# A set-attention and feed-forward kernel: the chunk products of the first attention half made eight visits later, its exponential two visits later, and a chooser that links the parts of a late chain and scores its last visit

## The chip, the cores and the metric

The kernel runs on one core of a Trainium2 chip. The metric is the device time of one execution in microseconds, the median over runs. A core has five engines with an instruction stream each: TensorE (PE, matrix products, with its weight loads as PEld), VectorE (DVE), ScalarE (ACT), GpSimd (POOL) and SyncE (SP), which issues most of the DMA transfers here. Each stream runs in the order in which it was written, and the streams meet through semaphores.

## The reference

An array x of 4 batches x 12,480 tokens x 128 channels goes through an induced set attention, and the result, 49,920 tokens, through a feed-forward layer:

```python
def mab(q, kv):
    s = scale * (q @ kv.transpose(0, 2, 1))
    s = s - s.max(-1, keepdims=True)
    a = np.exp(s)
    a /= a.sum(-1, keepdims=True) + 1e-09
    return a @ kv
h = mab(I, x)            # 32 inducing points attend to all tokens of a batch
y = mab(x, h)            # each token attends to the 32 rows of h
hid = y @ w_in           # 128 -> 2048
g = np.maximum(hid, 0.0) + alpha * np.minimum(hid, 0.0)
out = g @ w_out          # 2048 -> 128
```

The first `mab` needs a maximum and a sum over a whole batch before anything of the second can start. The second and the feed-forward layer work token by token.

## The kernel before

**Visits.** The heavy part is the feed-forward layer. A block is 4 tiles of 128 tokens (512 tokens), and the 2048 hidden channels are done in 4 visits of 512 channels, so a block takes 4 visits. There are 390 visits, numbered 0 to 389: 96 for each batch, and 6 for the tokens left over. In a visit (`visit`, L834 and after) PE makes four products `hh` of 128 channels x 512 tokens (L848; the 32 rows of h are folded into the weights as `HW`, so that four products of 32 rows run side by side). Each `hh` fills one of PSUM's eight banks. ACT (L861) or DVE (L863) applies the ReLU and writes it as `gt` in bf16, r = 0 to 3. After the next visit's four `hh`, PE multiplies the four `gt` of the visit before with W1 into a sum `bp` (`second`, L874, sixteen products). The linear part of the PReLU is added for two blocks at once (L901, every eighth visit). When a block's sum is complete, ACT (L927) or DVE (L929) copies it to `ob`, and SP sends it out (L934).

**Side work.** While the visits of batch b run, two other things are made between them. One is the second attention's weights for the next 2048 tokens of the same batch: scores (L684), their copy (L742, L744), maximum (L761), exponential on ACT (L728), sum, reciprocal, product and a DMA transpose `a<-rep` (L806). The other is the first attention of batch b+1, in seven pieces p = 0 to 6 (piece 1 is the short one of 192 tokens). For each piece: a load `xs`, a cast on POOL, a DMA transpose `xT` (L355), four score products (L378, `a_scores`), their scaled minimum on DVE (L417, L427), an exponential on ACT (L443, `e1T`), a factor for the running minimum (`fac`, L461), a DMA transpose of the exponentials (`e<-e1T`, L474), sixteen products with the tokens (L498, `a_h`) and their addition to the running sum `hs` on DVE (L512, L523). At the end of the seven pieces a chain closes the batch: `mg` (L542), `rb` (L551), `m` and `mf` (L558 to L564), `ex` on ACT (L577), `dx` and `den` on DVE (L587, L590), a product with `den` (L607), `rec`, a product with `hs` (L622), `hT` and the folded weights `HW` (L638, L645).

**Tables and the chooser.** The table near the end of the kernel names the visit after which each of these steps is written: `score`, `look` (the exponential; the transpose one visit and the factor two visits after), `join` (the products `a_h` and the addition). The class `Plan` then walks once over all visits before anything is written. For each visit it knows the side work's engine steps as a chain of (engine, ns) pairs, and it chooses with a beam of 64 states: which engine does which of the four ReLUs, which engine copies a finished block, whether a chain's ACT and DVE part is written at once or *late* (in the next visit, between its second and third ReLU), and which PSUM bank each product takes. `step` adds up a model of the engines' times with fixed prices (`RELU`, `COPY`, `FREE`, `SEM`), and `choose` keeps the states with the smallest estimated end of PE. The order of every engine is what these choices give. The lists `late` and `waits` carry the late parts from one visit to the next.

Of the kernel before, what the change touches and what calls it, by code (L numbers as in the profile page):

```python
# [30 lines left out]
def kernel(  # L31
# [55 lines left out]
    whole_pieces = pieces_of([(0, 0, ST), short, *((s, 0, ST) for s in range(1, NS - 1))])  # L87
# [26 lines left out]
    class Plan:  # L114
# [41 lines left out]
        def step(self, state, n, relus, ways):  # L156


            pe, a, v, e1, free, held, late = state
            cols, linear, accs, last, chains = self.visits[n]  # L160
            busy = {"a": a, "v": v}
            free, held, used = list(free), dict(held), []

            def take(pe):
                k = min(range(BANKS), key=lambda k: max(free[k] + self.SEM, pe))
                used.append(k)
                pe = max(pe, free[k] + self.SEM)
                free[k] = self.NEVER
                return pe, k

            hh, mine = [], []
            for r in range(R):
                k = min(range(BANKS), key=lambda k: free[k])
                used.append(k)
                mine.append(k)
                pe = max(pe, free[k] + self.SEM) + 4
                free[k] = self.NEVER
                hh.append(pe + cols * 0.417 + self.ARRIVE)
            out = []
            for r in range(R):  # L180
                if r == 2:
                    for k, ns, ready, bank in late:
                        busy[k] = max(busy[k], ready) + ns
                        if bank is not None:
                            free[bank] = busy[k] + 100
                lat, per, over = self.RELU[relus[r]]
                out.append(max(busy[relus[r]], hh[r]) + lat + per * cols)
                free[mine[r]] = out[r]
                busy[relus[r]] = out[r] - over
            pe += cols * 0.417  # L190
            for k in accs[0]:
                if k not in held:
                    pe, held[k] = take(pe)
            pe += linear + self.MODE
            for k in accs[1]:
                if k not in held:
                    pe, held[k] = take(pe)
            for r in range(R):
                pe = max(pe, e1[r] + self.SEM) + last * self.FREE
            waits = []  # L200
            for chain, way in zip(chains, ways):
                ready, bank = 0, None
                for kind, ns in chain:
                    if kind == "!":
                        continue
                    if kind == "free":
                        free[ns] = ready + 100
                        continue
                    if kind == "acc":
                        ready, bank = pe + self.ARRIVE, held.pop(ns)  # L210
                        continue
                    if kind in "ps":
                        if kind == "s":
                            pe, bank = take(pe)
                        pe += ns
                        ready = pe + self.ARRIVE
                        continue
                    k = way[0] if kind == "f" else kind
                    ns = self.COPY[k] if kind == "f" else ns
                    if way[-1:] == "l":  # L220
                        waits.append((k, ns, ready, bank))
                    else:
                        busy[k] = ready = max(busy[k], ready) + ns
                        if bank is not None:
                            free[bank] = ready + 100
                    bank = None
                if bank is not None:
                    free[bank] = ready + 600
            new = pe + self.MODE, busy["a"], busy["v"], tuple(out), tuple(free)
            return (*new, tuple(held.items()), tuple(waits)), used  # L230

        def choose(self):
# [3 lines left out]
            for n, (*_, chains) in enumerate(self.visits):  # L236
                ways = []
                for chain in chains:
                    kinds = [k for k, _ in chain]
                    if "f" in kinds:  # L240
                        ways.append([e + w for e in "av" for w in "nl"])
                    elif "!" in kinds or not {"a", "v"} & set(kinds):
                        ways.append([""])
                    else:
                        ways.append(["n", "l"])
                found = {}
                for state, path in beam:
                    for way in product(*ways):
                        for relu in relus:
                            new, used = self.step(state, n, relu, way)  # L250
                            at = new[0] + 390
                            over = max(new[1] - at, 0) + max(new[2] - at, 0)
                            over += sum(w[1] for w in new[6]) * 0.3
                            score = new[0] + 0.3 * over
                            ends = sorted(max(x - new[0], -200) for x in new[4])
                            key = (
                                *(int(x - new[0]) // 16 for x in new[1:3] + new[3]),
                                *(int(x) // 16 for x in ends if x < self.NEVER / 2),
                                new[6],
                            )  # L260
                            if key not in found or score < found[key][0]:
                                found[key] = (score, new, (path, relu + "".join(way), used))
                best = sorted(found.values(), key=lambda f: f[0])[: self.WIDTH]
                beam = [(new, path) for _, new, path in best]
# [8 lines left out]
    plan = Plan()  # L273
# [959 lines left out]
    end = State()  # L1233
# [27 lines left out]

    for b, s, nt in groups[1:]:
        n = first[b, s]
        when = [n - 23, n - 19, n - 16, n - 14, n - 13, n - 11, n - 9, n - 6]
        if (b, s) == (0, 1):
            when = [0, 2, 3, 6, 7, 9, 9, 9]
        if (b, s) == (0, 2):
# [32 lines left out]
    for b in range(B - 1):  # L1300
# [3 lines left out]
        for p, pc in enumerate(whole_pieces):  # L1304
            m = n + (8 * (p - 1 + (not b and p > 2)) if p > 1 else p)
            load, cast, turn = m - 3, m + 6, m + 8
            score = m + 15 if p > 1 else n + 16
            look = score + 1 + (p == 1)
            join = m + (24 if p == whole_pieces[-1].k else 23) if p > 1 else n + (31 if p else 23)
            if not b:  # L1310
                load, cast, turn = {
# [1 line left out]
                }.get(p, (load, cast, turn))  # L1313
                score, look = (score, look) if p > 1 else (score + 4, look + 4)
                join = n + 31 if p < 2 else n + 39 if p < 3 else join
            f = pc.full
            if load >= 0:
                at(load, on, b + 1, a_load, pc)
# [32 lines left out]
    for n, (blk, i) in enumerate(visits):  # L1351
# [3 lines left out]
        if i == 0 and n > NV:  # L1355
# [6 lines left out]
        plan.visits.append(  # L1362
            (blk.nt * blk.per * P, cost, (both, [before.k] if n else []), nt, chains)
        )
    plan.choose()

    prev = None
# [49 lines left out]
```

## Time and profile before

| | |
|---|---|
| median of 3 runs | 591.42 us (591.18 to 591.59) |
| the profiled execution | 593.02 us, of which the span of instructions 591.1 us |
| PE busy | 580.7 us, 98% of the span |
| PEld busy | 436.2 us, 74% |
| DVE busy | 534.4 us, 90% |
| ACT busy | 536.8 us, 91% |
| POOL busy | 217.2 us, 37% |
| granted TensorE clock | full speed in all slices |

How to read it: the busy share of PE counts each product until its modelled end, so small waits between products hide in it. They show better in the starts of the `hh` products of successive visits. The last group of sixteen L874 products of a visit starts about a third of a microsecond after its `hh`, and the next `hh` follow about a microsecond later. A visit that carries side work on PE is longer by that work.

### The profile page before, as it was taken

What the parts mean: (1) busy time and instruction counts of PE and PEld (TensorE: products, weight loads), DVE (VectorE), ACT (ScalarE), POOL (GpSimd) and SP (SyncE); (2) the same over time, 40 slices, a digit from 0 to 9 for tenths busy, and PEclk for the clock granted to TensorE, in tenths of its full rate; (3) what the DMA queues carried; (4) which work ended last, traced back from release to release, by engine and by line L of the source; (5) the groups of instructions that cost most, each with busy time, mean ns of one, the idle gap of its engine ahead of it and who ended that gap; (6) DMA issues with size and microseconds to landing.
All of it is one profiled execution on the core that took longest, in us unless ns stands there. A gap on an engine that the chain in (4) does not pass through costs nothing.

```text
span 591.1 us, 23015 instructions
## 1 busy us (share of the span) xinstructions
PE 580.7 (98%) x9443; PEld 436.2 (74%) x9443; DVE 534.4 (90%) x974; ACT 536.8 (91%) x1085; POOL 217.2 (37%) x259
## 2 busy tenths in 40 slices
PE   7899999999999999999999999999999999999997
PEld 3577777777777777777777777777777777777776
DVE  5799999988998998999999899999999999999996
ACT  5699999999999999999998999999999998999986
POOL 3575552523325426313226256124034134144110
PEclk9999999999999999999999999999999999999999
DMA  8786799734188899432256999741331331441321
GB/s 334 252 213 169 153 256 217 116 91 74 38 240 185 184 205 222 103 82 70 77 151 176 216 216 221 143 99 38 92 75 54 91 81 48 118 85 58 91 69 48
DMA packets 121964, 80.56 MB, mean 136 GB/s; under 512 B 103761, under 2 KB 105729, under 8 KB 118785
## 3 DMA queue, kind: packets, MB, share of 16 engines
q1 hardware_dynamic: 121632, 78.99, 56.0%
q8 instruction: 74, 1.21, 0.8%
q14 instruction: 34, 0.27, 0.1%
q10 hardware_dynamic: 224, 0.09, 0.1%
HBM read 28.07 MB, written 25.56 MB: 91 GB/s over the span
## 4 chain that ended last, share of the span: by engine, by line
PE 94%; DMA 3%; POOL 1%; DVE 0%; ACT 0%; issue 0%; DVEq 0%; SPq 0%; POOLq 0%
PE bp L874 66%; PE hh L848 22%; DMA xs<-in_x_dram 3%; PE bp L901 2%; PE hh L684 2%; PE hh L498 1%; PE hh L378 1%; POOL xn L348 0%; PE bp L1000 0%; PE hh L638 0%; DVEq L1412 0%; PE hh L607 0%; PE hh L622 0%; PE hh L1033 0%; PE hh L819 0%
## 5 line engine op out<-in xcount | busy, mean ns | idle before, releaser
L861 ACT ACTIVATE gt<-hh 128x512 bf16<-128x512 f32 x854 | 455.2, 606 | 34.3 <-PE hh L848 29.4
L863 DVE TENSOR_SCALAR gt<-hh 128x512 bf16<-128x512 f32 x706 | 453.4, 683 | 24.5 <-PE hh L848 13.2
L874 PE MATMUL bp<-W,gt 128*128 128x128 bf16 x6240 | 417.2, 220 | 0.7 <-DVE gt L863 0.7
L874 PEld LDWEIGHTS <-gt 128*128 128x128 bf16 x6240 | 349.3, 98 | 85.0 <-issue 76.5
L848 PE MATMUL hh<-a,HW 32*128 32x512 bf16 (+2 forms) x1664 | 156.0, 370 | 0.5 <-DVE a L827 0.5
L798 POOL TENSOR_TENSOR rep<-e,rc 128x2048 bf16<-128x2048 f32 (+2 forms) x26 | 84.8, 3265 | 23.0 <-DVE rc L789 22.6
L766 POOL TENSOR_TENSOR e<-e,smx 128x512 f32<-128x512 f32 (+1 forms) x24 | 24.6, 1027 | 154.6 <-ACT gt L861 79.4
L848 PEld LDWEIGHTS <-HW 32*128 32x128 bf16 x1664 | 40.4, 91 | 42.0 <-issue 5.9
L752 POOL TENSOR_TENSOR t<-e 128x256 f32<-128x256 f32 (+1 forms) x24 | 17.2, 718 | 144.1 <-ACT e L728 144.1
L927 ACT COPY ob<-bp 128x512 f32<-128x512 f32 (+1 forms) x63 | 36.9, 586 | 4.6 <-PE bp L874 1.7
L752 POOL TENSOR_TENSOR t<-t 128x128 f32<-128x128 f32 (+3 forms) x100 | 30.5, 305 | 7.8
L331 POOL CAST xn<-xs 128x2048 bf16<-128x2048 f32 x17 | 32.1, 1891 | 1.3 <-DMA xs<-in_x_dram 0.7
L929 DVE COPY ob<-bp 128x512 f32<-128x512 f32 x31 | 21.2, 684 | 5.2 <-PE bp L874 5.2
L417 DVE TENSOR_SCALAR_CACHE_REDUCE s<-hh 128x512 f32<-128x512 f32 (+2 forms) x29 | 17.9, 619 | 2.2 <-PE hh L378 1.9
L901 PEld LDWEIGHTS <-a 32*128 32x128 bf16 x392 | 14.9, 93 | 5.8 <-issue 0.2
L901 PE MATMUL bp<-HA,a 32*128 32x128 bf16 x392 | 19.1, 214 | 0.0
L443 ACT ACTIVATE e1T<-s,rm 128x512 bf16<-128x512 f32 (+1 forms) x25 | 17.9, 718 | 1.1 <-DVE rm L427 1.0
L761 DVE TENSOR_REDUCE smx<-e 128x16 f32<-128x512 f32 (+1 forms) x24 | 15.9, 661 | 0.0
L728 ACT ACTIVATE e<-e 128x512 f32<-128x512 f32 (+1 forms) x24 | 15.0, 624 | 0.0
L742 ACT COPY e<-hh 128x512 f32<-128x512 f32 (+1 forms) x22 | 13.4, 610 | 0.0
L684 PE MATMUL hh<-hT,xT 128*128 128x32 bf16 x372 | 13.0, 176 | 0.0
L523 DVE SCALAR_TENSOR_TENSOR hs<-hs,fac,hh 128x128 f32<-128x128 f32 (+1 forms) x21 | 7.2, 344 | 6.0 <-PE hh L498 5.3
(117 smaller groups left out, 195.2 us busy)
## 6 DMA issues: line engine op xcount, KB each, us to landing
out_dram<-ob SPq DMA_DIRECT2D x97, 256.0 KB, 2.5
xs<-in_x_dram SPq DMA_DIRECT2D x23, 1024.0 KB, 6.4
xs<-in_x_dram SPq DMA_DIRECT2D x2, 512.0 KB, 8.4
w_in_f<-in_moe_w_in_dram SPq DMA_DIRECT2D x1, 1024.0 KB, 9.9
a<-rep SPq DMA_TRANSPOSE x27, 4.7
xs_left<-in_x_dram SPq DMA_DIRECT2D x4, 96.0 KB, 5.8
xT<-xn SPq DMA_TRANSPOSE x18, 6.6
e<-e1T SPq DMA_TRANSPOSE x18, 3.0
```

What stands on the lines that cost most here:

```text
L331: nc.gpsimd.tensor_copy(out=st.xn[s][:], in_=xs[:])
L684: nc.tensor.matmul(ps[w, t, :], st.xT[:, tile0[s] + t, w], hTs[b][:], start=True, stop=True)
L752: nc.gpsimd.tensor_tensor(out=t[:, :n], in0=src[:, :n, :w], in1=src[:, :n, w : 2 * w], op=ADD)
L766: nc.gpsimd.tensor_tensor(out=st.e2[s][:, :n], in0=st.e2[s][:, :n], in1=st.m2[s][:, :n].unsqueeze(2).broadcast_to([P, n, M]), op=SUB,)
L798: nc.gpsimd.tensor_tensor(out=st.rep[s][:, ts], in0=st.e2[s][:, ts].unsqueeze(2).broadcast_to([P, n, R, M]), in1=rc[:, ts].unsqueeze(2).un ...
L848: nc.tensor.matmul(hh[:, q * cols + w.start : q * cols + w.stop], HWs[b][rows, v * P : (v + 1) * P], a2[rows, t0 : t0 + nt, :].rearrange(" ...
L861: nc.scalar.activation(out=gt[:, :cols], in_=hh[:, :cols], func=RELU)
L863: nc.vector.tensor_relu(gt[:, :cols], hh[:, :cols])
L874: nc.tensor.matmul(blk.acc[:, t * C : (t + 1) * C], gt[:, (q * nt + t) * P : (q * nt + t + 1) * P], W1[:, k, :], start=(not blk.begun), st ...
L901: nc.tensor.matmul(blk.acc[w, t * C : (t + 1) * C], blk.a2[rows, blk.t0 + t, w], HAs[b][rows, :], start=(not blk.begun and t == 0), stop=F ...
L927: nc.scalar.copy(out=ob[:, :nt], in_=acc)
L929: nc.vector.tensor_copy(out=ob[:, :nt], in_=acc)
```

## The change

Four things change.

1. In `step`, a chain that is written late has several parts on different engines. Each part used to be placed as soon as its engine was free. Now a part after the first (`linked`) starts, in the model, no earlier than the part before it has ended.
2. In `choose`, the last visit's states are scored by the time at which PE would finish the last block's products, one ReLU after the other, instead of by the ordinary score. `plan.end` is the number of products for each ReLU there (4).
3. The piece table moves. The exponential (`look`) goes from one visit after the scores to three. For pieces 2 and up the products `a_h` (`join`) go from `m + 23` to `m + 31`, that is from eight visits behind the piece's scores to sixteen. The last piece stays at `m + 24`, and the last but one shares its visit (`m + 32` of the piece before is the same visit). In batches 1 and 2, piece 0's products move to the visit of piece 1's, and the short piece 1 is scored three visits later, apart from piece 0.
4. The maximum over the second attention's scores (`when[1]`, L761) goes from 19 to 20 visits ahead of its use.

No computation is added or removed. Over the whole kernel the chooser now puts 834 ReLUs on ACT and 726 on DVE (854 and 706 before), and 89 block copies on ACT and 5 on DVE (63 and 31 before).

```diff
                 if r == 2:
-                    for k, ns, ready, bank in late:
-                        busy[k] = max(busy[k], ready) + ns
+                    done = 0
+                    for k, ns, ready, bank, linked in late:
+                        done = max(busy[k], ready, done if linked else 0) + ns
+                        busy[k] = done
                         if bank is not None:
                             free[bank] = busy[k] + 100
...
-                ready, bank = 0, None
+                ready, bank, linked = 0, None, False
...
                     if way[-1:] == "l":
-                        waits.append((k, ns, ready, bank))
+                        waits.append((k, ns, ready, bank, linked))
+                        linked = True
...
                             score = new[0] + 0.3 * over
+                            if n == len(self.visits) - 1:
+                                score = new[0] - self.MODE
+                                for ready in new[3]:
+                                    score = max(score, ready + self.SEM) + self.end * self.FREE
...
-        when = [n - 23, n - 19, n - 16, n - 14, n - 13, n - 11, n - 9, n - 6]
+        when = [n - 23, n - 20, n - 16, n - 14, n - 13, n - 11, n - 9, n - 6]
...
             score = m + 15 if p > 1 else n + 16
-            look = score + 1 + (p == 1)
+            look = score + 3 + 1 * (p == 1)
             join = m + (24 if p == whole_pieces[-1].k else 23) if p > 1 else n + (31 if p else 23)
...
+            if p == 1 and b:
+                score, look = score + 3, look + 3
+            end = whole_pieces[-1].k
+            if p > 1:
+                join = m + (24 if p == end else 32 if p == end - 1 else 31)
+            elif b:
+                join = n + 31
...
+    plan.end = visits[-1][0].nt * visits[-1][0].per
     plan.choose()
```

Three places show what this does to the order. In the changed kernel the line numbers behind the first hunks are seven higher, and from the piece table on up to fifteen, so L861 becomes L868 and L587 becomes L594.

The first place is DVE at the end of batch 0, visits 64 to 70, where the chain of `ex` (ACT), `dx` and `den` (DVE) closes batch 1's attention. Before:

```order
L558 TENSOR_REDUCE m_3454<-hh 128x1
L560 TENSOR_TENSOR m_3454<-m_3454,rm 128x1
L863 TENSOR_SCALAR gt<-hh 128x512 x4
L929 COPY ob<-bp 128x512
L587 TENSOR_TENSOR dx<-ex,da 128x7
L590 TENSOR_REDUCE den<-dx 128x1
L863 TENSOR_SCALAR gt<-hh 128x512
L789 RECIPROCAL rc_3583<-den_3502 128x16
```

The same place on DVE in the changed kernel:

```order
L565 TENSOR_REDUCE m_3448<-hh 128x1
L567 TENSOR_TENSOR m_3448<-m_3448,rm 128x1
L870 TENSOR_SCALAR gt<-hh 128x512 x6
L594 TENSOR_TENSOR dx<-ex,da 128x7
L597 TENSOR_REDUCE den<-dx 128x1
L796 RECIPROCAL rc_3565<-den_3483 128x16
L870 TENSOR_SCALAR gt<-hh 128x512 x2
```

Two ReLUs of visit 69 now stand ahead of `dx` and `den` on DVE, and the block copy has gone to ACT, where it stands just ahead of `ex`.

The second place is ACT in batch 1, from the piece scored in visit 126 to the next one (visits 127 to 137). Before:

```order
L443 ACTIVATE e1T,da<-s_5821,rm 128x512
L861 ACTIVATE gt<-hh 128x512 x7
L461 ACTIVATE fac<-rm 128x1
L728 ACTIVATE e_5611<-e_5611 128x512
L861 ACTIVATE gt<-hh 128x512 x4
L927 COPY ob<-bp 128x512
L861 ACTIVATE gt<-hh 128x512 x10
L443 ACTIVATE e1T,da<-s_6145,rm 128x512
```

The same place on ACT in the changed kernel:

```order
L934 COPY ob<-bp 128x512
L868 ACTIVATE gt<-hh 128x512 x2
L450 ACTIVATE e1T,da<-s_5803,rm 128x512
L868 ACTIVATE gt<-hh 128x512 x4
L735 ACTIVATE e_5589<-e_5589 128x512
L868 ACTIVATE gt<-hh 128x512 x2
L468 ACTIVATE fac<-rm 128x1
L868 ACTIVATE gt<-hh 128x512 x11
L934 COPY ob<-bp 128x512
L868 ACTIVATE gt<-hh 128x512
L450 ACTIVATE e1T,da<-s_6127,rm 128x512
```

The exponential moved from visit 127 to visit 129, the block copy that DVE made there (L929) came to ACT, and ACT now does three ReLUs of visit 127, in which DVE does one.

The third place is ACT at the end of the program, visits 386 to 389 and the last two copies. Before:

```order
L927 COPY ob<-bp 128x512
L861 ACTIVATE gt<-hh 128x512 x8
L927 COPY ob<-bp 128x512
L861 ACTIVATE gt<-hh 128x512 x2
L927 COPY ob<-bp 128x256
L940 DMA out_dram<-ob 64x2x128
```

The same place on ACT in the changed kernel:

```order
L934 COPY ob<-bp 128x512
L868 ACTIVATE gt<-hh 128x512 x11
L934 COPY ob<-bp 128x512
L934 COPY ob<-bp 128x256
L947 DMA out_dram<-ob 64x2x128
```

The last visit's ReLUs r = 0 and 1 were on DVE and are on ACT, r = 2 and 3 the other way round, and the copy of the last full block stands behind ACT's two ReLUs of that visit instead of ahead of them.

## The prediction

> **What bounds the kernel now.** I read the page's busy times first, then the time of each batch (the view by stretches of time), then the starts of PE's products in the timeline.
>
> ```profile
> PE 580.7 (98%) x9443; PEld 436.2 (74%) x9443; DVE 534.4 (90%) x974; ACT 536.8 (91%) x1085; POOL 217.2 (37%) x259
> PE 94%; DMA 3%; POOL 1%; DVE 0%; ACT 0%; issue 0%; DVEq 0%; SPq 0%; POOLq 0%
> 169.72:307.92 138.20, 138.20 (x2251) 104.03 (x2249) 127.11 (x230) 129.41 (x264) 52.51 (x57) 1.00 0.65 146
> 307.92:445.60 137.68, 137.68 (x2251) 103.92 (x2250) 127.23 (x230) 129.18 (x264) 52.37 (x55) 1.00 0.64 141
> 445.60:577.39 131.79, 131.79 (x2091) 100.43 (x2090) 122.90 (x199) 120.83 (x233) 37.42 (x48) 1.00 0.30 76
> ```
>
> PE holds the chain of waits, and the clock granted is 1.00. The last three rows are the 96 visits of batches 1, 2 and 3. Batch 3 carries no side work for a next batch, so 131.79 us is what 96 visits cost without it. Batches 1 and 2 have the same products (2251 in both) and yet differ by 0.52 us, so PE waits in them, although its busy time is modelled as full. The waits show between the starts of successive `hh` (L848):
>
> ```profile
> 216.00 0.39 PE L848 MATMUL hh<-a,HW 32*128 32x512 bf16 x4
> 216.33 1.24 PE L874 MATMUL bp<-W,gt 128*128 128x128 bf16 x16
> 217.50 0.39 PE L848 MATMUL hh<-a,HW 32*128 32x512 bf16 x4
> 218.83 0.50 PE L848 MATMUL hh<-a,HW 32*128 32x512 bf16 x4
> 220.26 0.40 PE L848 MATMUL hh<-a,HW 32*128 32x512 bf16 x4
> ...
> 224.46 0.65 PE L848 MATMUL hh<-a,HW 32*128 32x512 bf16 x4
> 226.67 0.39 PE L848 MATMUL hh<-a,HW 32*128 32x512 bf16 x4
> ```
>
> The visit from 217.50 to 218.83 takes 1.33 us; that is a visit without waits, and nearly all of the 390 are like it. The one from 216.00 takes 1.50: its sixteen L874 products last 1.24 instead of 1.07, since the last four wait for a `gt`. The one from 218.83 takes 1.43, and its four `hh` last 0.50 instead of 0.39: the fourth waits for a bank. The one from 224.46 takes 2.21 with scores and a piece's products in it, where the others of that kind take 1.88, and its `hh` last 0.65. So PE waits 0.17, 0.10 and 0.33 us here. The reason stands on DVE and ACT:
>
> ```profile
> 214.34 0.78 DVE L523 SCALAR_TENSOR_TENSOR hs<-hs,fac,hh 32x128 f32<-32x128 f32 x2
> 215.83 3.07 DVE L863 TENSOR_SCALAR gt<-hh 128x512 bf16<-128x512 f32 x5
> 218.82 0.68 DVE L929 COPY ob<-bp 128x512 f32<-128x512 f32 x1
> 216.13 0.72 ACT L443 ACTIVATE e1T<-s,rm 128x512 bf16<-128x512 f32 x1
> 216.83 3.71 ACT L861 ACTIVATE gt<-hh 128x512 bf16<-128x512 f32 x7
> ```
>
> From 214.34 to 215.83 DVE does sums, minimum and scores, so its ReLUs come late: the five behind one another take 3.07 us, a new one every 0.60, and the second, which that visit's last products need, ends at 215.83 + 0.60 + 0.68 = 217.11. ACT cannot help, since the exponential fills 216.13 to 216.83 (its ReLUs follow one another at 0.49). With seven ReLUs in 3.71 us ACT then works without a pause, and the lateness lasts until the next visit with slack.
>
> I went through all 390 starts in this way, against the shortest visit with the same side work. From the first exponential to the end of batch 2 the waits that lie in the scores-and-exponential stretches are: in batch 0 0.12 at 101.53 and 0.12 at 124.83; in batch 1 0.17 at 194.94, 0.22 at 196.44, the three above, and 0.12 at 241.10; in batch 2 0.17 at 333.10, 0.08 at 334.59, 0.16 at 354.02, 0.10 at 356.84 and 0.13 at 378.78. That is thirteen waits, 0.24 + 1.11 + 0.64 = 1.99 us, of which these rows show the first and the largest left:
>
> ```profile
> 101.53 0.52 PE L848 MATMUL hh<-a,HW 32*128 32x512 bf16 x4
> 102.99 0.40 PE L848 MATMUL hh<-a,HW 32*128 32x512 bf16 x4
> 196.44 0.62 PE L848 MATMUL hh<-a,HW 32*128 32x512 bf16 x4
> 197.99 0.44 PE L848 MATMUL hh<-a,HW 32*128 32x512 bf16 x4
> ```
>
> A single wait is larger than all these. It stands at the end of batch 0:
>
> ```profile
> 132.11 0.30 ACT L577 ACTIVATE ex<-rm 128x7 f32<-128x7 f32 x1
> 132.44 0.17 DVE L587 TENSOR_TENSOR dx<-ex,da 128x7 f32<-128x7 f32 x1 [0.95 <-ACT ex L577]
> 132.01 0.40 PE L848 MATMUL hh<-a,HW 32*128 32x512 bf16 x4
> 133.46 0.62 PE L874 MATMUL bp<-W,gt 128*128 128x128 bf16 x8 [0.50 <-DVE gt L863]
> 134.21 0.40 PE L848 MATMUL hh<-a,HW 32*128 32x512 bf16 x4
> ```
>
> DVE stood idle for 0.95 us, because `dx` was ahead of two ReLUs in its stream and needed `ex`, which ACT reached only behind its own ReLUs. The visit took 2.20 us, against 1.52 for the visits with the same L607 work in batches 1 and 2: 0.67 us.
>
> **The change part by part.**
>
> *The linked chain.* `dx` and `den` now stand behind visit 69's first two ReLUs on DVE, about 1.2 us of work, and `ex` stands ahead of visit 69's ReLUs on ACT. From ACT's order I add up: visit 68's two ReLUs (0.98), `fac`, a block copy (0.48, the spacing of such copies) and `ex` end about 0.8 us after visit 69's `hh` are there, and DVE needs 1.2 us for the two ReLUs, so `dx` waits for nothing. `den` is needed by L607 only a visit later. Gain 0.67 us; ends 0.4 (if ACT's copy comes late) and 0.67. What is late next there is a bank for the fourth `hh` of visit 69, some 0.1 us, which I put into the remainder below.
>
> *Exponential three visits behind the scores.* The two bursts, DVE's 1.5 us with the scores and ACT's 0.7 with the exponential, no longer meet. In the place shown, ACT takes three ReLUs of the first visit and DVE one; so DVE's last ReLU ends one ReLU earlier, 217.11 - 0.60 = 216.51, ahead of its use at 217.0, and ACT's third ends at 216.13 + 0.60 = 216.73, also ahead. The wait of 0.17 goes. In the next two visits DVE has two ReLUs each (1.2 us in 1.33) and no copy, so the bank waited for at 218.83 is free in time. The copy and the exponential are then on ACT within two visits: four ReLUs, a copy and the exponential are 4 x 0.49 + 0.48 + 0.71 = 3.15 us against 2.65, so ACT is half a microsecond late at that point, with DVE on time. Two more banks are free there, because no scores and no piece's products are waiting to be read, and this covers it. In the first stretch of batches 1 and 2, the waits at 194.94 and 333.10 come with two exponentials in two visits; these are now three visits apart (visits 115 and 118). So I take all thirteen waits as gone, 1.99 us; ends 0.8 and 1.99.
>
> *New waits.* ACT's half microsecond comes at about five visits in each of three batches. Adding up the engines at one of them (visits 126 to 134) leaves one bank late by about 0.07 us, at visit 133. Six such places, plus the 0.1 above, are 0.5 us; ends 0 and 1.5.
>
> *Products eight visits later.* These are the same sixteen L498 products and one L523 for each piece, in as many visits, and nearly always beside a score. The visit with the first lone score becomes shorter by what the last visit, which now has two pieces, becomes longer. I price this at nothing on PE. The sum `hs` is needed by L622 three visits after the last two pieces (one visit after in batch 0), and one more addition of 0.35 us lies in between. The buffers hold: six for the transposed exponentials, of which two or three are in use. On SP the transposes L474 now stand behind the `a<-rep` transposes instead of ahead of them. They have time: 12 visits instead of 6 before use for most pieces. For the last piece five visits are left, and I come back to it.
>
> *The lone score of the short piece.* It goes to a visit of its own in batches 1 and 2.
>
> ```profile
> 190.54 0.40 PE L848 MATMUL hh<-a,HW 32*128 32x512 bf16 x4
> 191.87 0.47 PE L378 MATMUL hh<-xT,IT 128*32 128x512 bf16 x5
> 192.27 0.39 PE L848 MATMUL hh<-a,HW 32*128 32x512 bf16 x4
> 63.61 0.40 PE L378 MATMUL hh<-xT,IT 128*32 128x512 bf16 x4
> 63.94 0.40 PE L848 MATMUL hh<-a,HW 32*128 32x512 bf16 x4
> ```
>
> Five scores take 0.40 us until the next `hh`, four take 0.33, so the fifth costs 0.07 beside others. Alone it costs between 0.07 and 0.33. I take the middle, 0.20; less the 0.07 saved this is 0.13 in each of two batches, 0.26 us, with ends 0 and 0.52. The Trainium skill says in "TensorEngine Tiling (Array Packing)", Key Properties, that a change of the tiling mode, and not only of the tile, drains TensorE. By that rule the lone score pays what four do, and the sum would have 0.52 in place of 0.26. The rows lean to the rule, since four scores and five differ by so little, but no run here shows a lone score.
>
> *The last visit.* PE's last products wait for a ReLU on DVE:
>
> ```profile
> 584.62 0.59 ACT L927 COPY ob<-bp 128x512 f32<-128x512 f32 x1 [0.34 <-PE bp L874]
> 585.05 1.29 DVE L863 TENSOR_SCALAR gt<-hh 128x512 bf16<-128x512 f32 x2 [0.43 <-PE hh L848]
> 585.23 0.38 SPq L937 DMA_DIRECT2D out_dram<-ob  x1
> 586.40 0.84 PE L874 MATMUL bp<-W,gt 128*128 128x128 bf16 x12 [0.20 <-DVE gt L863]
> 587.68 0.72 ACTq L940 DMA_DIRECT2D out_dram<-ob  x1
> DMA to landing us min/median/max: 2.2/2.4/3.8
> ```
>
> With r = 0 and 1 on ACT, the second is ready at 585.05 + 0.49 + 0.60 = 586.14 instead of 586.34, so the last products start 0.2 us earlier: gain 0.20. Against it, the copy of the last full block comes behind two ReLUs, so its transfer is issued at about 586.65 instead of 585.23. It was the slow one of the three (3.8 us to landing), and at 3.8 us again it would land at 590.5, later than the last transfer does now (587.68 + 2.4 = 590.1): a loss of 0.4. With the usual 2.4 it is hidden. I take the gain of 0.2; ends -0.2 and +0.4.
>
> *POOL and `when[1]`.* The maximum one visit earlier frees DVE in the next visit; POOL is 37% busy, and nothing waits for it sooner. Nothing.
>
> **The sum.** -0.67 - 1.99 + 0.5 + 0.26 - 0.20 = -2.10 us. Against the profiled execution (593.02 us, span 591.1) this gives 590.9; that execution was 1.6 us slower than the median of the runs, so for the median I take 591.42 - 2.10 = 589.3 us.
>
> **The rivals.**
>
> *The waits only move.* The work of ACT and DVE is the same, 90% and 91% of the span, so a burst taken apart could be late elsewhere. With 2.0 us of new waits in place of 0.5 the sum is -0.6: 590.8 us. For it speaks that ACT gets 26 copies and loses 20 ReLUs, 26 x 0.48 - 20 x 0.49 = 2.7 us more, against it that DVE loses (26 - 20) x 0.60 = 3.6, and that batch 3, with two engines nearly as full (122.90 and 120.83 of 131.79), has no wait.
>
> *ACT becomes the bound at the moved exponentials.* The mechanism is the half microsecond above: if no bank covers it, PE waits up to 0.4 us at each of fifteen places, 6.0 instead of 0.5 us of new waits, and the sum is +3.4: 594.8 us. From 0.17 us a place on the gain is gone (15 x 0.17 = 2.6), from 0.25 on (3.8, sum +1.2) the kernel is slower. For it: at 216.13 an exponential between ReLUs did go with waits of 0.17 and 0.10. Against: those needed DVE to be late too.
>
> *The last piece's products come too late.* In batches 1 and 2 the exponential of the last piece moves by two visits, and its transpose behind `a<-rep` on SP. Such a transpose took 7.8 us to issue when a load was under way (second row below), otherwise 1.2.
>
> ```profile
> 220.87 1.22 SPq L474 DMA_TRANSPOSE e<-e1T  x1
> 212.98 7.79 SPq L355 DMA_TRANSPOSE xT<-xn  x1
> ```
>
> No load stands there in SP's stream, so this would cost at most a microsecond in each of two batches, and the sum is about 0: 591.3 us. I count it with "the waits only move".
>
> **How the numbers follow.** About 0.2% (1.2 us) is what a measurement of this kernel can tell from no change, so faster begins below 590.2. The forecast, 589.3, with its own range 588.6 to 590.2, has 0.62. The waits that only move, around 590.8, with the late transpose, have 0.26 and end within 0.2%. ACT as the bound, 594.8, has 0.12. So faster 0.62, same 0.26, slower 0.12. The low end is all waits gone, no new ones, the lone score at nothing and the last visit at 0.2: -2.86, 588.5. The high end leaves out the ACT rival beyond its beginning and takes the moved waits with the lone score at 0.33 and the late last transfer: 591.42 - 0.6 + 0.26 + 0.6 = 591.7. As some of the rival lies just above, I take 592.0.
>
> **What the profile of the changed kernel would show.** `dx` without an idle 0.95 us ahead of it; no L874 group in the scores stretches above 1.1 us and no `hh` group above 0.42; a lone L378 of 192 columns at visits 114 and 210 and its price; the last products 0.2 us sooner; batches 1 and 2 near 137.2 us. The forecast is wrong if `hh` groups behind the moved exponentials last 0.5 us or more, or if L498 of the last pieces waits for its transpose.

## The result and the profile after

The changed kernel takes 589.64 us (median of six runs, 588.9 to 591.3), the kernel before 591.61 in six runs beside it. The ratio is 0.9965, with a 95% interval of 0.9949 to 0.9982: faster by 0.35%, about 2.0 us. The profiled execution took 591.30 us with a span of 589.2, against 593.02 and 591.1 before.

Busy times, the chain of waits and the stretches of time of batches 0 to 3 in the changed kernel (start and end of the stretch, its length, then the busy time of PE, PEld, DVE, ACT and POOL, the granted clock, and the DMA share and rate):

```profile
PE 580.1 (98%) x9443; PEld 436.6 (74%) x9443; DVE 532.4 (90%) x968; ACT 538.1 (91%) x1091; POOL 216.8 (37%) x259
PE 95%; DMA 3%; POOL 1%; DVE 0%; issue 0%; SPq 0%; ACT 0%; DVEq 0%; POOLq 0%
31.00:169.41 138.41, 138.41 (x2286) 104.92 (x2286) 127.61 (x234) 131.18 (x269) 59.87 (x74) 1.00 0.69 154
169.41:306.64 137.23, 137.23 (x2252) 104.09 (x2252) 126.56 (x228) 129.71 (x266) 52.42 (x57) 1.00 0.63 147
306.64:443.86 137.22, 137.22 (x2252) 104.07 (x2251) 126.54 (x228) 129.69 (x266) 52.36 (x55) 1.00 0.64 141
443.86:575.64 131.78, 131.78 (x2090) 100.43 (x2088) 123.78 (x200) 120.56 (x232) 37.34 (x48) 1.00 0.29 76
```

Busy times and chain tell nothing of the gain: PE reads 98% in both. The stretches do. Batches 1 and 2 fell from 138.20 and 137.68 to 137.23 and 137.22 and now are equal, batch 0 fell from 139.22 to 138.41 (between the starts of visits 0 and 96), and batch 3, which has no side work for a next batch, stayed at 131.78. Together the starts of visits 0 and 384 came 2.24 us closer; from the last visit's start to the end of the span it is 6.42 instead of 6.64.

The timeline of PE in the changed kernel at the place that the prediction showed (visits 127 to 131):

```profile
213.74 0.40 PE L855 MATMUL hh<-a,HW 32*128 32x512 bf16 x4
215.06 0.40 PE L855 MATMUL hh<-a,HW 32*128 32x512 bf16 x4
215.39 1.08 PE L881 MATMUL bp<-W,gt 128*128 128x128 bf16 x16
216.40 0.40 PE L855 MATMUL hh<-a,HW 32*128 32x512 bf16 x4
217.73 0.40 PE L855 MATMUL hh<-a,HW 32*128 32x512 bf16 x4
219.06 0.40 PE L855 MATMUL hh<-a,HW 32*128 32x512 bf16 x4
```

Four visits of 1.32 to 1.34 us stand where there were 1.50 and 1.43 among them; the sixteen products take 1.08 (1.24 before), and no `hh` group lasts over 0.40. The end of batch 0, on PE, DVE and ACT:

```profile
132.04 0.40 PE L855 MATMUL hh<-a,HW 32*128 32x512 bf16 x4
133.56 0.40 PE L855 MATMUL hh<-a,HW 32*128 32x512 bf16 x4
134.89 0.72 PE L505 MATMUL hh<-xn,e 128*32 128x128 bf16 x32
135.54 0.40 PE L855 MATMUL hh<-a,HW 32*128 32x512 bf16 x4
...
128.79 3.67 DVE L870 TENSOR_SCALAR gt<-hh 128x512 bf16<-128x512 f32 x6
132.38 0.16 DVE L594 TENSOR_TENSOR dx<-ex,da 128x7 f32<-128x7 f32 x1
131.57 0.33 ACT L584 ACTIVATE ex<-rm 128x7 f32<-128x7 f32 x1
```

`ex` ends at 131.90, `dx` starts right behind DVE's ReLUs and waits for nothing, and the visit from 132.04 takes 1.52 us instead of 2.20. The next one, with 32 products `a_h` (L505) instead of sixteen, takes 1.98 instead of 1.66.

The tail, in the timeline of PE's weight loads, ACT and SP, and in the page's DMA issues:

```profile
583.29 1.08 ACT L868 ACTIVATE gt<-hh 128x512 bf16<-128x512 f32 x2 [0.27 <-PE hh L855]
584.26 0.59 ACT L934 COPY ob<-bp 128x512 f32<-128x512 f32 x1
584.43 0.67 PEld L881 LDWEIGHTS <-gt 128*128 128x128 bf16 x12 [0.20 <-ACT gt L868]
584.88 0.38 SPq L944 DMA_DIRECT2D out_dram<-ob  x1
585.72 0.72 ACTq L947 DMA_DIRECT2D out_dram<-ob  x1
DMA to landing us min/median/max: 2.2/2.3/2.4
```

The last full block's copy now stands behind two ReLUs, and its transfer is issued at 584.88, 0.84 us ahead of the final one at 585.72. None of the last three transfers takes over 2.4 us any more (3.8 before), so it lands before the last.

### The profile page after: what moved, and what is told of

Same layout as the page of the kernel before. It is cut to its first block, busy times and chain, and to the rows that moved or that the text cites. A ratio compares the mean times of both kernels' runs of the same rounds, so it can differ in the third digit from the quotient of the medians.

```text
span 589.2 us, 22996 instructions
## 1 busy us (share of the span) xinstructions
PE 580.1 (98%) x9443; PEld 436.6 (74%) x9443; DVE 532.4 (90%) x968; ACT 538.1 (91%) x1091; POOL 216.8 (37%) x259
## 4 chain that ended last, share of the span: by engine, by line
PE 95%; DMA 3%; POOL 1%; DVE 0%; issue 0%; SPq 0%; ACT 0%; DVEq 0%; POOLq 0%
PE bp L881 66%; PE hh L855 22%; DMA xs<-in_x_dram 3%; PE bp L908 2%; PE hh L691 2%; PE hh L505 1%; PE hh L385 1%; POOL xn L355 0%; PE bp L1007 0%; PE hh L645 0%; PE hh L614 0%; PE hh L629 0%; PE hh L1040 0%; PE hh L826 0%; SPq L326 0%
## 5 line engine op out<-in xcount | busy, mean ns | idle before, releaser
L870 DVE TENSOR_SCALAR gt<-hh 128x512 bf16<-128x512 f32 x726 | 465.2, 684 | 29.5 <-PE hh L855 15.9
L868 ACT ACTIVATE gt<-hh 128x512 bf16<-128x512 f32 x834 | 448.3, 615 | 32.4 <-PE hh L855 27.4
L855 PE MATMUL hh<-a,HW 32*128 32x512 bf16 (+2 forms) x1664 | 154.1, 371 | 0.5 <-DVE a L834 0.5
L934 ACT COPY ob<-bp 128x512 f32<-128x512 f32 (+1 forms) x89 | 53.0, 596 | 2.8 <-PE bp L881 0.5
L691 PEld LDWEIGHTS <-xT 128*128 128x128 bf16 x384 | 12.1, 96 | 0.2
```

The source lines that it names most:

```text
L691: nc.tensor.matmul(ps[w, t, :], st.xT[:, tile0[s] + t, w], hTs[b][:], start=True, stop=True)
L855: nc.tensor.matmul(hh[:, q * cols + w.start : q * cols + w.stop], HWs[b][rows, v * P : (v + 1) * P], a2[rows, t0 : t0 + nt, :].rearrange(" ...
L868: nc.scalar.activation(out=gt[:, :cols], in_=hh[:, :cols], func=RELU)
L870: nc.vector.tensor_relu(gt[:, :cols], hh[:, :cols])
L934: nc.scalar.copy(out=ob[:, :nt], in_=acc)
```

## The account by visits

I subtracted, visit by visit, the spacing of the `hh` starts before from that after. What differs, in us:

| term | predicted | measured |
|---|---|---|
| the wait of `dx` (visit 70) | -0.67 | -0.67 |
| the thirteen waits in the scores stretches | -1.99 | -1.99 |
| waits that I had not counted (visits 22, 26, 100, 195) | none | -0.30 |
| new waits: visits 66 and 68 0.06 each, 150 and 246 0.11 each, six of about 0.04; less 0.03 at visit 69 | +0.5 | +0.52 |
| products moved (46, 118, 214 shorter by 0.22 each, 126 and 222 by 0.05; 71 longer by 0.31, 159 and 255 by 0.22) | 0 | -0.01 |
| lone score: 2 x 0.18, less 2 x 0.07 | +0.26 | +0.22 |
| last visit | -0.20 | -0.22 |

These add up to -2.45, and from the start of visit 0 to the end of the span the two traces differ by 2.24 + 0.22 = 2.46. So the sum stood, but an account of places does not say which edit moved each of them. The experiments do.

## The experiments

Visits are numbered 0 to 389. "By visits" is the time between the starts of visits 0 and 384, which leaves out the start and the tail. A ratio given beside two medians is not their quotient, so the two differ a little.

### The linked chain alone

The kernel before with only the first edit:

```diff
-                    for k, ns, ready, bank in late:
-                        busy[k] = max(busy[k], ready) + ns
+                    done = 0
+                    for k, ns, ready, bank, linked in late:
+                        done = max(busy[k], ready, done if linked else 0) + ns
+                        busy[k] = done
...
-                        waits.append((k, ns, ready, bank))
+                        waits.append((k, ns, ready, bank, linked))
+                        linked = True
```

> The kernel before with the linked chains alone (table and last visit as before). Theory A (each part of the change has its own place): only the wait at the end of batch 0 goes, the visit with L607 falls from 2.20 to about 1.52 us, and the thirteen waits in the scores stretches stay (1.11 us of them in batch 1): 0.7 us less, 590.9. Theory B (most of the gain is the chooser's better view of late chains, everywhere): the waits of the scores stretches shrink too, by half or more, and the time is 590.0 or less.

Measured: 590.47 us against 591.30, ratio 0.9985 (0.9977 to 0.9994); by visits -0.95. Visit 70 lost its 0.67, visit 71 gained 0.14, visit 100 lost 0.09. All waits of the scores stretches stayed but one, that at visit 134. The rows of this kernel beside those of the prediction:

```profile
216.97 0.51 PE L851 MATMUL hh<-a,HW 32*128 32x512 bf16 x4
...
222.60 0.40 PE L851 MATMUL hh<-a,HW 32*128 32x512 bf16 x4
224.48 0.40 PE L851 MATMUL hh<-a,HW 32*128 32x512 bf16 x4
```

The `hh` group of 0.51 is there as before; the visit from 222.60 takes 1.88 where it took 2.21. Through all of batch 1 every engine has its instructions in the same order in the two programs, so the 0.33 us at that visit belongs neither to the exponential nor to the order of the engines. The last section shows where it begins. Without it the linked chain alone is worth 0.62 us by visits.

### The last visit alone

```diff
+                            if n == len(self.visits) - 1:
+                                score = new[0] - self.MODE
+                                for ready in new[3]:
+                                    score = max(score, ready + self.SEM) + self.end * self.FREE
```

> The kernel before with the last visit's score alone. Theory A: every visit but the last two is as before, PE's last products end 0.2 us sooner, and the time is 591.3, which timing can hardly tell from before; the profile shows it in the length of the last visit (6.64 us from its first product to the end of the span, 6.4 with the change). Rival: the copy of the last full block is issued so late that its transfer lands last, and the last visit takes 6.9 or more.

Measured: 590.93 us against 591.30, ratio 0.9998 (0.9989 to 1.0008). All visits but the last are as before, and from the last visit to the end of the span it is 6.41 instead of 6.64. The block's transfer, issued later, landed in 2.3 us. The 0.2 us shows in the trace and is too small for the times.

### The table without the chooser's edits

The changed kernel with edits 1 and 2 taken back; the piece table and `when[1]` stay.

```diff
-                    for k, ns, ready, bank, linked in late:
-                        done = max(busy[k], ready, done if linked else 0) + ns
-                        busy[k] = done
+                    for k, ns, ready, bank in late:
+                        busy[k] = max(busy[k], ready) + ns
...
-    plan.end = visits[-1][0].nt * visits[-1][0].per
```

> The changed kernel with the chooser's two edits taken back, so only the table is moved. Theory A: the thirteen waits in the scores stretches go (1.99 us), the lone score adds 0.3, and the wait at dx stays if the chooser again puts dx late and unlinked: about 590.0, with batches 1 and 2 at 137.2 us each in the profile. Theory B: the table alone gives at most 0.6 us: 591.0.

Measured: 591.64 us against 591.30, ratio 1.0005 (0.9996 to 1.0014): the table alone gives nothing. By visits the thirteen waits are gone as in the changed kernel, but the wait of `dx` is now in each of batches 0 to 2: visit 70 takes 2.16, and visits 158 and 254, which took 1.52 before, take 2.36. Visit 158, on PE and on DVE:

```profile
256.99 0.39 PE L848 MATMUL hh<-a,HW 32*128 32x512 bf16 x4
258.41 0.62 PE L874 MATMUL bp<-W,gt 128*128 128x128 bf16 x8 [0.48 <-DVE gt L863]
259.35 0.40 PE L848 MATMUL hh<-a,HW 32*128 32x512 bf16 x4
...
257.40 0.17 DVE L587 TENSOR_TENSOR dx<-ex,da 128x7 f32<-128x7 f32 x1 [0.87 <-ACT ex L577]
```

It is the same pattern that cost 0.67 us at one place before: DVE stands 0.87 us at `dx`, its ReLUs are late, and PE waits. The chooser, which does not know that `dx` follows `ex`, steps into it three times with the new table. So the linked chain is worth 0.95 us on the old table by visits, and on the new one 0.64 + 0.84 + 0.84 = 2.3 at these three places (2.16 over all visits). Theory A expected that wait to stay at its one place, not to come three times; the time fits theory B, but for this reason and not because the table leaves the thirteen waits. The new table needs the linked chain; the linked chain gains something without it, and the table adds 1.29 us by visits on top of it.

### The later exponential without the later products

The kernel before with one line of the table:

```diff
-            look = score + 1 + (p == 1)
+            look = score + 3 + 1 * (p == 1)
```

> The kernel before with the exponential three visits behind the scores, and nothing else: the products stay eight visits behind, so that four visits (5.3 us) are left from the issue of the transpose to its use instead of six. Theory A: the later exponential takes away most of the thirteen waits (1.0 to 2.0 us), but the products of some pieces now wait for their transpose, whose issue stands behind the transposes of xT and of rep: 0 to 1 us in each batch, 589.9 to 591.9. Rival C (the move of the products is what the exponential's move cannot do without): the products wait 1 us or more in every batch and the time is over 593.

Measured: 596.43 us against 591.30, ratio 1.0078 (1.0064 to 1.0091), 4.6 us slower by the ratio. The profiled execution was the fastest of the five, 594.92, and is 3.67 slower by visits: 2.02 in batch 1, 1.59 in batch 2 and nothing in batch 0. So rival C was right, though not for every batch. Ten waits of the scores stretches went or shrank, as the theory says (49, 65, 115, 128, 130, 145, 211, 224, 226, 241), and larger ones came: visit 126 took 4.27 instead of 2.03, visit 222 3.45, visit 230 2.30. Visit 126 on PE, and SP's own DMA queue:

```profile
214.34 0.41 PE L498 MATMUL hh<-xn,e 128*32 128x128 bf16 x16 [2.10 <-DMA e<-e1T]
207.50 2.98 SPq L806 DMA_TRANSPOSE a<-rep  x1
210.57 1.28 SPq L474 DMA_TRANSPOSE e<-e1T  x1
```

The transpose of the exponentials is issued only behind the one of `a<-rep`, which holds SP for 2.98 us, and PE stands in front of the products until 214.34. With the exponential two visits later and the products at their old place, this transpose has no time left. With the table alone it is issued in the same visit, 125, behind the same `a<-rep` transpose, but its products stand at visit 134, and no product of a piece waits for its transpose. The move by eight visits, which I priced at nothing, is what makes the later exponential possible.

### The exponential back to one visit, all else changed

```diff
-            look = score + 3 + 1 * (p == 1)
+            look = score + 1 + 1 * (p == 1)
```

> The changed kernel with the exponential back at one visit behind the scores (products sixteen behind, linked chains and last visit as changed). Theory A (the waits in the scores stretches come from the exponential meeting DVE's burst): they come back, 1.2 to 2.0 us over batches 0 to 2, and the time is 590.8 to 591.6 against 589.6 for the changed kernel. Rival D (the room that the later products and the linked chains give to the chooser is enough): at most 0.5 us comes back, 590.1 or less.

Measured: 590.85 us against 591.49, ratio 0.9992 (0.9983 to 1.0002); by visits batches 0 to 2 are 0.39, 0.39 and 0.33 longer than in the changed kernel, 1.11 us together. Waits of 0.12 to 0.13 us came back at visits 49, 65, 130, 145, 226 and 241, and one of 0.12 at 129 and 225, one visit behind the old ones at 128 and 224. Those at 114, 115, 210, 211 and 134 did not come back. The small waits at 22 and 26 did come back, and waits of 0.10 appeared at 122 and 218. On PE, the place of the prediction (visits 129 and 130), with DVE and ACT just ahead of it, and one place in batch 3:

```profile
214.51 0.40 PE L855 MATMUL hh<-a,HW 32*128 32x512 bf16 x4
215.96 0.53 PE L855 MATMUL hh<-a,HW 32*128 32x512 bf16 x4
217.42 0.40 PE L855 MATMUL hh<-a,HW 32*128 32x512 bf16 x4
213.10 6.06 DVE L870 TENSOR_SCALAR gt<-hh 128x512 bf16<-128x512 f32 x10
214.26 0.74 ACT L450 ACTIVATE e1T<-s,rm 128x512 bf16<-128x512 f32 x1
...
571.75 0.63 PE L855 MATMUL hh<-a,HW 32*128 32x512 bf16 x4
573.39 0.40 PE L855 MATMUL hh<-a,HW 32*128 32x512 bf16 x4
```

The `hh` groups of 0.5 us and the visits of 1.45 are back with the exponential next to the scores: DVE's ten ReLUs begin late, at 213.10, and the exponential fills ACT from 214.26. So the place of the exponential is shown as the cause of eight of the thirteen waits, 1.02 of the 1.99 us. The wait at 571.75 is another matter: it is 0.31 us in batch 3, 0.63 for the `hh`, and no side work is near it. The time lies in theory A's range with the help of this wait; the 1.11 us are a little less than expected.

### The short piece scored beside piece 0

```diff
-            if p == 1 and b:
-                score, look = score + 3, look + 3
```

> The changed kernel with the short piece scored beside piece 0 again in batches 1 and 2, and its exponential one visit behind that of piece 0. Theory A: the lone score's visit (1.50 us) falls to 1.33 and the pair's visit grows from 1.66 to 1.73, 0.10 in each batch; but two exponentials in two visits bring the waits of the first stretch back (0.2 to 0.4 in each batch): 589.6 to 590.2. Rival: those waits stay away, because the exponentials are three visits behind the scores: 589.4.

Measured: 589.85 us against 591.49, ratio 0.9974 (0.9965 to 0.9983); by visits 0.20 and 0.19 slower than the changed kernel in batches 1 and 2, and 0.31 in batch 3 at one visit (310). In batch 1 the five scores cost 0.07 more at visit 111, visit 114 takes 1.42 instead of 1.51, and visit 134 2.02 instead of 1.88. So scoring the short piece alone costs 0.18 in its own visit, but a wait of 0.09 stands there otherwise, and elsewhere it saves more. So theory A had the direction: waits came back, but only 0.09 of them in the first stretch's visit 114 and 0.14 at 134, and of the 0.70 us by visits 0.31 is at visit 310, which it did not have. The interval overlaps that of the changed kernel: by the times alone the two are not told apart. PE in batch 3, at a visit without side work on PE:

```profile
472.34 0.63 PE L855 MATMUL hh<-a,HW 32*128 32x512 bf16 x4
472.90 1.14 PE L881 MATMUL bp<-W,gt 128*128 128x128 bf16 x16
```

### The exponential doubled, after and before

In both kernels the exponential of each piece of batches 1 to 3 is done twice with the same operands. The 21 additional ones (18 of about 0.72 us and 3 short ones of 0.45, with the reads of their sums) add 14.6 us to ACT's busy time in the changed kernel and 15.1 in the one before; the values stay the same. This is the test of the rival that ACT becomes the bound.

```diff
+            for _ in range(1 + (st.b > 0)):
                 nc.scalar.activation(
                     out=e1T[:parts, : pc.q * P].rearrange("m (j t) -> m j t", j=pc.q)[:, :, : pc.last],
```

> The changed kernel with the exponential of each piece of batches 1 to 3 made twice (the same values written again; the chooser is not told), so ACT has about 0.7 us more at 21 places, 15 us in all. Theory A (the burst is taken apart, and banks cover a late ACT): about half of it is absorbed, 4 to 9 us more than the changed kernel, and clearly less than the same edit costs the kernel before. Rival E (ACT is already at its limit at the moved exponentials): 10 us or more, and as much as in the kernel before.

> The kernel before with the exponential of each piece of batches 1 to 3 made twice in the same way. Theory A: there the exponential meets DVE's burst and nothing covers it, so 9 to 14 us more than the kernel before. Rival E: the same cost as in the changed kernel.

Measured: 602.68 us in the changed kernel and 607.22 in the one before, one run each. By visits 13.27 us more in the changed kernel, 91% of the work added, and 15.53 in the one before, all of it. So theory A, half of it absorbed, was wrong. Rival E had the size right; the cost is 2.3 us less than in the kernel before, not the same, and there it is above the 9 to 14 us expected. The stretch of batch 1 in each:

```profile
171.88:313.71 141.83, 139.92 (x2251) 104.57 (x2249) 127.05 (x228) 134.51 (x280) 52.52 (x57) 1.00 0.61 143
```

```profile
173.70:316.95 143.25, 140.40 (x2251) 104.16 (x2250) 127.48 (x230) 134.49 (x278) 52.40 (x57) 1.00 0.60 142
```

ACT has 134.5 us of work in both, well below the length of the stretch, and yet PE pays nearly all of what was added. The mean cover at such a place is (14.6 - 13.27) / 21 = 0.06 us in the changed kernel and nothing in the one before. The chooser's table of costs does not know of the second exponential, so this is the slack of a fixed order and not of one chosen anew.

### The maximum back by one visit

```diff
-        when = [n - 23, n - 20, n - 16, n - 14, n - 13, n - 11, n - 9, n - 6]
+        when = [n - 23, n - 19, n - 16, n - 14, n - 13, n - 11, n - 9, n - 6]
```

> The changed kernel with the maximum over the second attention's scores back at 19 visits ahead of its use. Theory A: worth nothing by itself, since batch 3 had no wait with 19 either: at most 0.3 us from the changed kernel (589.6), in either direction. Rival F: together with the moved exponential DVE's maximum falls into a full visit, and 0.1 us comes back at each of about eighteen places: 591.

Measured: 589.0 us against 591.5, ratio 0.9956 (0.994 to 0.9973), which the times do not tell from the changed kernel. By visits it is 0.26 us slower (0.11 at 54, 0.06 at 83, 0.05 each at 158 and 254). Pricing the edit at nothing was right within what can be measured.

## Why the prediction was right, point by point

The forecast of 589.3 us was missed by 0.3, and its sum of -2.10 stands against -1.97 in the medians and -2.46 in the traces. This is less of a proof than it seems: some of its steps were right in size for reasons that hold only in part, and 0.33 us of the gain is luck.

**The linked chain, -0.67.** Right as a place: `dx` waits for nothing, and the visit takes 1.52. Not seen was that the new table alone would bring the same wait into all three batches, so that on the new table the edit carries 2.16 us by visits. I had read the order of the finished program, where the edit's work was already done, and could read from it only what had been there before.

**Thirteen waits, -1.99.** All went, and the place shown behaves as worked out (products 1.08, `hh` 0.40). The cause was "the two bursts no longer meet" for all. The kernel with the exponential back shows that cause for eight of them, 1.02 us, two of which came back a visit later. The waits at 114, 115, 210 and 211 (0.64 us) do not come back with it, and with the short piece beside piece 0 only 0.09 does at 114 and at 210. The later exponential in the kernel before took away those at 115 and 211 and left 0.14 at 114 and 210. So the two edits share these four waits. The 0.33 us at 224.46 was ascribed wrongly: it follows a DVE ReLU that waited 0.55 us for ACT's block copy (last section), and it went with the linked chain alone, where all engines keep their order. Two small variants of the changed kernel, with the exponential back and with the short piece beside piece 0, have such a wait in batch 3; that the changed kernel has none was luck.

**New waits, +0.5.** Measured 0.52, but none of it where I had reckoned it. Visit 133, with its late bank, takes 1.33 us, a visit without waits. Of the new waits 0.34 us are at visits 66, 68, 150 and 246, and the six of 0.03 to 0.04 are at 43, 59, 123, 139, 219 and 235. In those six the `hh` group lasts 0.39 and the products are longer, as here at visit 123, because the fifth of the sixteen waits for a ReLU of DVE and not for a bank:

```profile
207.85 1.11 PE L881 MATMUL bp<-W,gt 128*128 128x128 bf16 x16
```

Those six and the two at 150 and 246 are there too in the kernel before with the exponential alone moved, so they belong to that move. The size was right by luck.

**Products eight visits later, nothing.** Right as a sum (-0.01). Three visits became 0.22 shorter, three longer, and the pair of 32 products costs 0.22 in batches 1 and 2 but 0.31 in batch 0, where 0.09 of it is missing with the table alone and so comes with the linked chain. Yet "nothing" hid that this edit is a condition for the later exponential: without it the kernel is 4.6 us slower, by the transpose on SP that I had feared for the last piece alone.

**The lone score, +0.26.** The rows of the changed kernel settle what the rows before could not:

```profile
194.44 0.39 PE L855 MATMUL hh<-a,HW 32*128 32x512 bf16 x4
195.77 0.26 PE L385 MATMUL hh<-xT,IT 128*32 128x192 bf16 x1
195.96 0.39 PE L855 MATMUL hh<-a,HW 32*128 32x512 bf16 x4
```

From its start to the next `hh` it is 0.19 us, and the visit takes 1.51, 0.18 over a plain one. The middle of 0.07 and 0.33 was near. By the rule that I cited from the Trainium skill, "TensorEngine Tiling (Array Packing)", Key Properties, taken as a price that does not depend on the number of products, it would have been 0.33; one score pays 0.18 and four pay 0.33, so a part at most is fixed.

**The last visit, -0.20.** Measured -0.22, and -0.23 with the edit alone. The slow transfer did not come: it took 2.3 to 2.4 us to landing in the six programs that issue it later, against 3.3 to 3.8 in the other five.

**What I had not counted, -0.30.** Small waits at visits 22, 26, 100 and 195, below or outside what I had listed. Those at 22 and 26 come back with the exponential, so it is the cause of half of this.

**The rivals.** That the waits only move did not happen in the changed kernel, but it is what the table alone does, with 591.64 us, and by the mechanism named for the old place and not by the burst moved elsewhere. ACT as the bound did not happen; the doubled exponential shows how near it was. I argued that two more free banks cover ACT's half microsecond. No wait came at most of these places, and an ACT later by 0.7 us found 0.06 us of cover on average, so a chance of 0.12 was not too much. That it is the banks that cover is not shown: no run changes their number. The late transpose is real where the products are not moved, and was not seen in the changed kernel.

## What to carry to other kernels

A table that moves work and the model that orders from it are one change: here the table alone gave 1.0005 and the model alone 0.9985, while both with a further small edit gave 0.9965, so each is to be tried with the other before it is judged. Of the gain of the model alone 0.33 us is the wait at visit 134, which no edit aimed at. Waits of an engine whose busy share reads 98% show in the spacing of its recurring groups, and a place found so still needs an experiment for its cause. To learn how much cover an operation has, double it: a busy share of 91% on ACT let one expect room, and the kernels paid 91% and all of what was added.

## What the runs showed of the hardware that was not expected

**A wait of a third of a microsecond with one signature.** In five of the eleven programs one visit is 0.31 to 0.33 us longer: its `hh` group lasts 0.63 to 0.65 instead of 0.39, and the products behind it 1.14 instead of 1.07. It stands at visit 134 before, in the kernel with the last-visit score alone and with the doubled exponential before; at visit 382 with the exponential back, at 310 with the short piece beside piece 0; and in none of the other six. The last two places are in batch 3 and have no side work on PE near them. The traces show where it begins. The kernel before (L863), the linked chain alone (L866), the exponential back (DVE at 571.27) and the changed kernel (DVE at 572.16):

```profile
223.24 0.59 ACT L927 COPY ob<-bp 128x512 f32<-128x512 f32 x1
223.99 1.29 DVE L863 TENSOR_SCALAR gt<-hh 128x512 bf16<-128x512 f32 x2 [0.55 <-ACT ob L927]
221.38 0.59 ACT L930 COPY ob<-bp 128x512 f32<-128x512 f32 x1
221.76 1.29 DVE L866 TENSOR_SCALAR gt<-hh 128x512 bf16<-128x512 f32 x2 [0.18 <-PE hh L851]
571.27 3.90 DVE L870 TENSOR_SCALAR gt<-hh 128x512 bf16<-128x512 f32 x6 [0.54 <-ACT ob L934]
572.16 3.34 DVE L870 TENSOR_SCALAR gt<-hh 128x512 bf16<-128x512 f32 x5 [0.19 <-PE hh L855]
```

In each of the five, a ReLU on DVE in the visit before starts only when ACT's copy of a finished block has ended, after 0.53 to 0.55 us of idling, and the fourth `hh` of the long visit starts when that ReLU has ended. In no other place of the eleven traces does a ReLU on DVE show such a wait; with the linked chain alone it starts at 221.76, before the copy ends at 221.97. The order of every engine is the same in batch 1 of the first pair and in batch 3 of the second, so the order is not what differs. Why the ReLU waits for the copy in the one program and not in the other stays open; no run here was made for it.

**One score costs over half of four.** 0.18 us alone, 0.33 for four, 0.07 for a fifth beside four.

**The start varies more than the change.** The first visit began at 31.00 us in the profiled execution of the changed kernel, 30.51 before, and between 28.66 and 30.09 in the nine experiments, though no edit touches what is ahead of it and not all ran on the same chip. Single spans are therefore no measure for 2 us; the spacing of the visits is: batch 3 took 131.78 us in the changed kernel and 131.79 before, though the two spans began half a microsecond apart.
